# Three raw weight pieces and two stores go from SyncE's DMA queue to GpSimd's; a row load, a table part and two step A groups move to later pairs

## The chip, the cores and the metric

The kernel runs on one core of a Trainium2 chip. A core has a matrix engine (TensorE, PE in the profile), VectorE (DVE), ScalarE (ACT), GpSimd (POOL) and SyncE (SP, which here only issues transfers). Each engine works through its own instructions in order and waits for the others by semaphores. Transfers are issued by SP, ACT or POOL, each into a DMA queue of its own (q1, q10 and q0 in the profile), and all queues are served by the same 16 DMA engines. The metric is device time in microseconds (us); lower is better.

## The reference, cut to what matters

```python
X = np.fft.rfft(x, axis=1)                     # x: 4 x 3008 x 256
Yr = Xr @ w_r - Xi @ w_i + b_r                 # mixing of the 256 channels, per frequency
Yi = Xr @ w_i + Xi @ w_r + b_i
Y = soft_threshold(Yr, 0.01) + 1j * soft_threshold(Yi, 0.01)
y = np.fft.irfft(Y, n=3008, axis=1)            # 12032 tokens x 256
h = y @ w_in                                   # 256 -> 2048
g = np.maximum(h, 0.0) + alpha * np.minimum(h, 0.0)
out = g @ w_out                                # 2048 -> 256
```

## The kernel before, in words

The sequence length is factored as 3008 = 47 x 64, and each batch passes five steps. Step A (`a_load`, `a_mm`, `a_evac`) is a length 47 transform over rows of x. Step B (`b_load`, `b_mm`, `b_evac`) is the length 64 transform with a table `rb_s`. The mixing with w_r and w_i (`m_mm`, `m_evac`) follows, then the inverse transforms C (`c_mm`, `c_evac`, table `cf_s`) and D (`d_mm`). The 24 frequency slots are handled as 12 pairs. Behind the transforms stand the two large products with w_in and w_out, which take most of the time. This change touches only the first tenth of the program: the first batch, and what is loaded meanwhile.

The order of all work is written out by hand. A loop over t = 0 to 12 issues for each t: step B of pair t, `b_load` of pair t+3, the store of pair t-4, mixing of pair t-1, step C of pair t-3, and then extra work. The extra work has four parts that matter here.

- **Raw weight pieces.** w_in and w_out arrive as 16 pieces of 512 KB each (`conv_load`, line 257), w_in and w_out in turn; they are numbered 0 to 15 here. Three of them fit into the upper half of `cw_s`, so piece n+3 can be issued only when piece n has been read. `pump` then splits each piece into a high and a low part with some ten ACT and DVE instructions. L272 on ACT is the first to read a piece, L286 on ACT the last; L292 on DVE reads it too. From t = 2 on, three or four such groups are issued in each t.
- **Table parts.** `load_rb` (line 208) loads the table of step B: slots 4 to 11 during step A, 12 to 17 and 18 to 23 in the loop. Pair t needs slots 2t and 2t+1, so pair 6 is the first to need slots 12 to 17.
- **The next batch's step A.** `a_load(1, g)` loads 376 KB of x; its four matmuls for two groups are run with pair 4, or, in the change, with pair 6. `a_evac` on ACT copies each group out of PSUM, and `put` stores the results (192 KB each).
- **Step B's inputs.** Each `b_load` is two transfers of 128 KB issued by POOL; POOL also runs one small instruction (L511, writing `Xl`) for each pair, on which the mixing of that pair waits.

Everything that one engine issues is in program order, its transfers included: a transfer that waits for its buffer holds up the transfers behind it on that queue.

Of the kernel before, what the change touches and what calls it, by code (L numbers as in the profile page):

```python
# [96 lines left out]
def fft_mix_moe(ctx, tc, x, w_r, w_i, b_r, b_i, w_in, w_out, alpha, la, rb, lc, rd, lf, cf, sel, out):  # L97
    nc = tc.nc
# [61 lines left out]
    def half(h):  # L160
        t = const.tile([128, 2, FH * 2 * C], F32R, tag=f"half{h}", name=f"w{h}")
        wi_h[h] = t[:, 0].rearrange("p (w k f) -> p w k f", w=2, k=CT)
        wo_h[h] = t[:, 1].rearrange("p (m w f) -> p m w f", w=2, f=C)

    def load_tables():
        nc.sync.dma_start(out=rd_s, in_=rd)
        nc.sync.dma_start(out=alpha_s, in_=alpha.rearrange("(k p) -> p k", p=128))
# [39 lines left out]
    def load_rb(n0, n1, at=0):  # L207
        nc.sync.dma_start(out=rb_s[:, n0:n1], in_=rb[:, n0 + at:n1 + at])

    def load_cf(n0, n1):  # L210
        nc.gpsimd.dma_start(out=cf_s[:, n0:n1], in_=cf[:, n0:n1])
# [34 lines left out]
    conv_deep = [1]  # L246
    conv_raw, conv_old, conv_ops = [], [], []

    def conv_load():

        m, i = divmod(conv_m[0], 2)
        conv_m[0] += 1
        k = conv_m[0] % 3
        raw = cw_s[:, NSLOT + 8 * k:NSLOT + 8 * k + 8].rearrange("p (k n) f -> p k (n f)", k=2)
        raw = raw.rearrange("p k (n w) -> p k n w", w=2)
        src = w_out.bitcast(U32)[256 * m:256 * m + 256] if i else w_in.bitcast(U32)[:, 512 * m:512 * m + 512]
        nc.sync.dma_start(out=raw.rearrange("p k n w -> p k (n w)"), in_=src.rearrange("(k p) f -> p k f", p=128))
        conv_raw.append((raw, m, i))

    def conv_first(raw, m, i):  # L260
# [48 lines left out]
    def conv_fetch():  # L309
        assert not conv_ops  # L310
        while len(conv_raw) < conv_deep[0] and conv_m[0] < conv_m[1]:
            conv_load()

    def pump(n):

        while n > 0:
            if not conv_ops:
                conv_fetch()
                second = conv_second(*conv_old.pop()) if conv_old else []
                first = conv_first(*conv_raw.pop(0)) if conv_raw else []  # L320
                first, second = ([(op,) for op in ops] for ops in (first, second))
                if first and second:
                    conv_ops.extend([second[0] + first[0], first[1], second[1], second[2] + second[3] + first[2]])
                else:
                    conv_ops.extend(first + second)
                if not conv_ops:
                    return
            for op in conv_ops.pop(0):
                op()
            n -= 1  # L330
# [5 lines left out]
    def put(*queues):  # L336
        for n, (o, i) in enumerate(stores):
            (queues or (nc.sync,))[n % max(len(queues), 1)].dma_start(out=o, in_=i)
        stores.clear()
# [3 lines left out]
    def a_load(b, g):  # L343

        if g == 0:
            ad[b] = dram.tile([NQ, R, C], F32, tag="ad", name=f"ad{b}")
        src = x[b].rearrange("(p r) c -> p r c", r=R)[:, 4 * g:4 * g + 4]
        if b == 0:
            ts = [x_s[:, 4 * g:4 * g + 4]]
        elif b == 1 and g in X1_TAGS:  # L350
            tags = X1_TAGS[g]
            ts = [work.tile([NP, 4 // len(tags), C], F32, tag=tag, name="xt", bufs={"Yl": None, "gl": 3}.get(tag, 1))
                  for tag in tags]
        else:
            ts = [work.tile([NP, 4, C], F32, tag="xt", name="xt")]
        if (b, g) == (0, 0):
            ts = [ts[0][:, 0:2], ts[0][:, 2:4]]
        n = 4 // len(ts)
        for i, t in enumerate(ts):

            for p in ((0, 80), (80, NP)):
                nc.sync.dma_start(out=t[slice(*p)], in_=src[slice(*p), n * i:n * i + n])
        xt[b, g] = ts
# [20 lines left out]
    def a_mm(b, g):  # L384
        ps = ps_f.tile([NQ, 2, C], F32, tag="f", name="ps_a")
        pa[b, g] = ps
        if b < 2:
            ts = x_rows(b, g)
            n = 2 // len(ts)
            for i, t in enumerate(ts):  # L390
                PE.matmul(ps[:, n * i:n * i + n], lf_s, t, start=True, stop=True)  # L391
            return
        hi, lo = xp.pop((b, g))
        PE.matmul(ps, la_s[:, 0], hi, start=True, stop=False)
        PE.matmul(ps, la_s[:, 1], hi, start=False, stop=False)
        PE.matmul(ps, la_s[:, 0], lo, start=False, stop=True)

    def a_evac(b, g):
        ps = pa.pop((b, g))
        if b == 0:  # L400
            st = a0_s[:, g]
        else:
            tag = A1_TAGS[g] if b == 1 and g < len(A1_TAGS) else "zst"
            st = work.tile([NQ, 2, C], F32, tag=tag, name="ast", bufs={"bt": 3, "zst": 3, "Yt": 1, "Yc": 1}.get(tag))
        if b == 0 and g % 2:
            V.tensor_copy(out=st, in_=ps)
        else:
            A.activation(out=st, in_=ps, func=AF.Copy)
        if b:
            stores.append((ad[b][:, 2 * g:2 * g + 2], st))  # L410
# [3 lines left out]
    def b_half(q, h):  # L414
        if h == 0:
            bt[0, q] = work.tile([128, 2, C], F32, tag="bt", name="bt", bufs=3)
        src = a0_s.rearrange("(w s q) (h g) r c -> q h w s (g r) c", w=4, s=2, h=2)[q, h]
        for k in range(2):
            (nc.sync if h else nc.gpsimd).dma_start(out=bt[0, q][64 * h:64 * h + 64, k], in_=src[:, k])

    def b_load(b, q):
        if (b, q) == (0, 2):
            t = work.tile([128, 2, C], F32, tag="Yc", name="bt2", bufs=1)
        else:
            t = work.tile([128, 2, C], F32, tag="bt", name="bt", bufs=3)
        if b == 0:
            src = a0_s.rearrange("(w s q) g r c -> q w s (g r) c", w=4, s=2)[q]
        else:
            src = ad[b].rearrange("(w s q) r c -> q w s r c", w=4, s=2)[q]

        for k in range(2):
            (nc.gpsimd if b == 0 else nc.sync).dma_start(out=t[:, k], in_=src[:, k])
        bt[b, q] = t
# [550 lines left out]
    NG = R // 2  # L984
    EARLY = 4
    FILL = 14
    C0 = 1
    PT = [0, 0, 3, 3, 3, 3, 3, 3, 3, 3, 3, 4]
    TAIL = [['me', 1], ['ce', 3], ['cm', 2], ['cm', 1], ['ce', 2], ['ce', 1], ['d'], ['f', 4], ['e'], ['f', 6]]
    WARM = 38  # L990
# [10 lines left out]
    with tc.manual_schedule():  # L1001
# [13 lines left out]
        for n, (b, g) in enumerate(seq):  # L1015
            a_mm(b, g)
            if n >= 1:
                a_evac(*seq[n - 1])
            if n == NG // 2:
                b_half(0, 0)  # L1020
                b_half(1, 0)
            if n == NG:
                b_half(0, 1)
                b_half(1, 1)
                load_rb(4, 12)
                for _ in range(C0):
                    conv_load()
                a_load(1, 1)
                bias_parts()
                b_load(0, 2)  # L1030
        a_evac(*seq[-1])
# [4 lines left out]
        def run(fn, q, *args):  # L1036
            if 0 <= q < NPAIR:
                fn(0, q, *args)
# [10 lines left out]
        for t in range(NPAIR + 1):  # L1049
            if t == 0:  # L1050
                first_pair()
            elif t > 1:
                run(b_mm, t)
            run(b_load, t + 3)
            run(c_evac, t - 4)
            if t > 1:
                run(b_evac, t)
            run(m_evac, t - 2)
            if t > 1:
                run(m_mm, t - 1, ps_h)  # L1060
            for g in range(2, EARLY) if t == 4 else ():
                a_mm(1, g)
                a_evac(1, g)
            if t:
                run(b_evac2, t)
            run(c_mm, t - 3)
            if t < NPAIR:
                pump(PT[min(t, len(PT) - 1)])
            if t in (3, 5):
                load_rb(3 * t + 3, 3 * t + 9)  # L1070
            if t in (0, 3, 6, 8):
                load_cf((t + 1) // 3 * 6, (t + 1) // 3 * 6 + 6)
            if t == 2:
                put()
                conv_load()
                conv_deep[0] = 2
            if t == 5:
                put()
            if t == 6:
                load_tables()  # L1080
            if 7 <= t < 12:
                a_load(1, t - 5)
            if t == NPAIR - 1:
                load_rb(0, 4)
            if t == 10:
                half(1)
                conv_m[1] = FT
# [160 lines left out]
        for k in range(len(spairs) + SLAG):  # L1248
# [7 lines left out]
            if k >= SLAG:  # L1256
                n, t = spairs[k - SLAG]
# [45 lines left out]
```

## Time and profile before

| | |
|---|---|
| median of 3 runs | 1335.99 us (1335.87 to 1336.71) |
| the profiled execution | 1338.1 us, of which the span from first to last instruction is 1336.0 us |
| granted TensorE clock, mean | 0.997 |
| PE / DVE / ACT / POOL busy | 1321.9 / 1046.0 / 732.7 / 352.8 us |
| bytes over the DMA queues | 89.74 MB |

The profiled execution took 2.1 us more than the median of the runs, about as much as lies outside its span. Places in the trace are given in us from the start of the span. Steps A to C of the first batch lie between 9 and 91 us, and the large products begin at about 104 us.

### The profile page before, as it was taken

The page shows a single profiled execution, that of the slowest core. Times are in us where ns is not written, and L with a number is a line of the kernel's source. Part 1 is how long each engine was busy: PE and PEld are TensorE (multiplying, and loading weights), DVE is VectorE, ACT ScalarE, POOL GpSimd, SP SyncE. Part 2 cuts the span into 40 slices and gives each one's busy share as a digit, 9 for nine tenths or more (in the row PEclk, how much of TensorE's full clock was granted, in tenths as well). Part 3 has the DMA queues.
Part 4 walks back from the last instruction along what each step waited for, and adds up shares of the span by engine and source line. Part 5 has one row for each costly group of instructions (what it writes and reads, how often), then busy time and mean ns, then how long its engine had stood idle before and what let it go on. Part 6 is the DMA issues. An engine that isn't in the chain of part 4 may idle for free.

```text
span 1336.0 us, 22138 instructions
## 1 busy us (share of the span) xinstructions
PE 1321.9 (99%) x7864; PEld 1156.1 (87%) x7864; DVE 1046.0 (78%) x1874; ACT 732.7 (55%) x1453; POOL 352.8 (26%) x337
## 2 busy tenths in 40 slices
PE   8999999999999999999999999999999999999998
PEld 5978878888888888888879888988898889888987
DVE  3666866777787877686878888888888888888885
ACT  3666654555455544444455555555555555555554
POOL 3403752212221222222222222222222222222222
PEclk9999999999999999999999999999999999999999
DMA  9984333432143322121101101110111011101000
GB/s 204 254 232 138 102 108 97 129 107 87 57 144 101 107 70 67 57 76 36 37 13 40 28 11 30 29 29 11 31 29 28 12 29 29 29 12 29 17 16 25
DMA packets 103759, 89.74 MB, mean 67 GB/s; under 512 B 62446, under 2 KB 85849, under 8 KB 103648
## 3 DMA queue, kind: packets, MB, share of 16 engines
q1 hardware_dynamic: 95744, 77.68, 20.7%
q0 software_dynamic: 4912, 7.76, 2.3%
q10 hardware_dynamic: 2992, 2.88, 0.7%
q8 instruction: 62, 1.02, 0.3%
q14 instruction: 49, 0.40, 0.1%
HBM read 50.76 MB, written 34.34 MB: 64 GB/s over the span
## 4 chain that ended last, share of the span: by engine, by line
PE 89%; DVE 4%; DMA 3%; ACT 1%; issue 1%; SPq 0%; ACTq 0%; DVEq 0%
PE ps_h L725 36%; PE ps_o L752 10%; PE ps_o L750 10%; PE ps_o L751 10%; PE ps_m L547 6%; PE ps_d L646 4%; PE ps_b L437 3%; PE ps_o L919 3%; PE ps_a L391 2%; DVE q L737 1%; PE ps_m L534 1%; DMA cw_s<-in_moe_w_out 1%; PE ps_c L615 1%; PE ps_c L616 1%; DMA rb_s<-tab_rb 1%
## 5 line engine op out<-in xcount | busy, mean ns | idle before, releaser
L725 PE MATMUL ps_h<-yh,w 128*128 128x512 f32 (+1 forms) x1472 | 492.5, 389 | 2.3 <-DVE q L737 1.4
L725 PEld LDWEIGHTS ps_h<-yh,w 128*128 128x128 f32 x1472 | 275.1, 188 | 58.2 <-DVE q L737 4.5
L725 PE MATMUL ps_h<-yl,w 128*128 128x512 f32 (+1 forms) x736 | 284.8, 387 | 0.0
L853 POOL TENSOR_TENSOR l<-t,h 128x512 fp32r<-128x512 f32 x98 | 126.9, 1295 | 448.8 <-ACT h L851 423.8
L824 DVE SCALAR_TENSOR_TENSOR sq<-sq,beta_s,ps_h 128x512 f32<-128x512 f32 (+1 forms) x240 | 166.2, 724 | 58.6 <-ACT sq L823 58.3
L739 ACT ACTIVATE gh<-q 128x512 fp32r<-128x512 f32 x144 | 91.0, 632 | 159.4 <-DVE q L737 159.4
L742 POOL TENSOR_TENSOR gl<-q,gh 128x512 fp32r<-128x512 f32 x69 | 93.5, 1355 | 270.9 <-ACT gh L739 216.1
L725 PEld LDWEIGHTS ps_h<-yl,w 128*128 128x128 f32 x736 | 138.9, 189 | 21.7 <-DVE yl L697 0.2
L737 DVE SCALAR_TENSOR_TENSOR q<-q,beta_s,ps_h 128x512 f32<-128x512 f32 x144 | 107.0, 743 | 59.3 <-ACT q L736 58.1
L823 ACT ACTIVATE sq<-ps_h 128x512 f32<-128x512 f32 (+1 forms) x240 | 132.0, 577 | 31.3 <-PE ps_h L725 27.9
L839 ACT ACTIVATE dh<-sq 128x768 fp32r<-128x768 f32 x98 | 83.0, 847 | 108.2 <-DVE sq L824 81.7
L736 ACT ACTIVATE q<-ps_h 128x512 f32<-128x512 f32 x144 | 85.3, 592 | 79.1 <-PE ps_h L725 76.9
L851 ACT ACTIVATE h<-t 128x512 fp32r<-128x512 f32 x98 | 62.0, 633 | 104.6 <-DVE t L849 102.5
L750 PE MATMUL ps_o<-gh,w 128*128 128x512 f32 x288 | 114.6, 398 | 0.0
L751 PE MATMUL ps_o<-gh,w 128*128 128x512 f32 x288 | 112.7, 391 | 0.0
L752 PE MATMUL ps_o<-gl,w 128*128 128x512 f32 x288 | 112.7, 391 | 0.0
L848 DVE TENSOR_TENSOR dl<-sq,dh 128x768 fp32r<-128x768 f32 x98 | 93.2, 951 | 0.0
L742 DVE TENSOR_TENSOR gl<-q,gh 128x512 fp32r<-128x512 f32 x75 | 59.2, 789 | 42.3 <-ACT gh L739 41.3
L752 PE MATMUL ps_o<-l,sw_a 128*128 128x256 f32 x294 | 82.7, 281 | 0.0
L750 PE MATMUL ps_o<-h,sw_a 128*128 128x256 f32 x294 | 82.0, 279 | 0.0
L845 DVE TENSOR_TENSOR t<-sq 128x512 f32<-128x512 f32 x98 | 67.7, 691 | 2.9
L852 DVE TENSOR_TENSOR l<-t,h 128x512 fp32r<-128x512 f32 x98 | 67.0, 684 | 0.0
(202 smaller groups left out, 2946.2 us busy)
## 6 DMA issues: line engine op xcount, KB each, us to landing
zt<-zd SPq DMA_DIRECT2D x32, 384.0 KB
zd<-zst SPq DMA_DIRECT2D x37, 256.0 KB
ad<-ast SPq DMA_DIRECT2D x48, 192.0 KB
bt<-ad SPq DMA_DIRECT2D x72, 128.0 KB
out<-oT SPq DMA_DIRECT2D x248, 32.0 KB
xt<-in_x SPq DMA_DIRECT2D x21, 320.0 KB
cw_s<-in_moe_w_in SPq DMA_DIRECT2D x8, 512.0 KB
cw_s<-in_moe_w_out SPq DMA_DIRECT2D x8, 512.0 KB
```

The lines of the kernel that those rows point to most:

```text
L725: PE.matmul(ps, wi_h[m // FH][:, w, ct, 128 * (m % FH):128 * (m % FH) + 128], a[ct][:, 0:n], start=(k == 0), stop=(k == 3 * CT - 1))
L736: A.activation(out=q, in_=ps, func=AF.Relu, scale=-1.0)
L737: V.scalar_tensor_tensor(out=q, in0=q, scalar=beta_s[:, m:m + 1], in1=ps, op0=ALU.mult, op1=ALU.add)
L739: A.activation(out=hi, in_=q, func=AF.Copy)
L742: return lambda: (V if by_v else G).tensor_tensor(out=lo, in0=q, in1=f(hi), op=ALU.subtract)
L750: PE.matmul(o, wh, gh, start=first, stop=False)
L751: PE.matmul(o, wl, gh, start=False, stop=False)
L752: PE.matmul(o, wh, gl, start=False, stop=last)
L823: A.activation(out=q[:, j], in_=ps, func=AF.Relu, scale=-1.0)
L824: V.scalar_tensor_tensor(out=q[:, j], in0=q[:, j], scalar=beta_s[:, m:m + 1], in1=ps, op0=ALU.mult, op1=ALU.add)
L848: V.tensor_tensor(out=dl, in0=q[:, HS:], in1=f(dh), op=ALU.subtract)
L853: G.tensor_tensor(out=l24, in0=t24, in1=f(h24), op=ALU.subtract)
```

## The change

Pieces 0, 1 and 2 are no longer issued by SP during and after step A, but by POOL, with pairs 1, 2 and 3. The two stores of the next batch's first step A groups go from SP at t = 2 to POOL at t = 3. `a_load(1, 1)` moves from step A to t = 4, and `load_rb(12, 18)` from t = 3 to t = 4, behind it; the matmuls of groups 2 and 3 move from t = 4 to t = 6, and their stores from t = 5 to t = 7. `load_rb(18, 24)` stays at t = 5. The number of bytes, matmuls and split operations is the same.

```diff
-    def conv_load():
+    def conv_load(queue=None):
...
-        nc.sync.dma_start(out=raw.rearrange("p k n w -> p k (n w)"), in_=src.rearrange("(k p) f -> p k f", p=128))
+        (queue or nc.sync).dma_start(out=raw.rearrange("p k n w -> p k (n w)"), in_=src.rearrange("(k p) f -> p k f", p=128))
...
                 load_rb(4, 12)
-                for _ in range(C0):
-                    conv_load()
-                a_load(1, 1)
                 bias_parts()
...
-            for g in range(2, EARLY) if t == 4 else ():
+            for g in range(2, EARLY) if t == 6 else ():
                 a_mm(1, g)
                 a_evac(1, g)
             if t:
                 run(b_evac2, t)
             run(c_mm, t - 3)
+            if t in (1, 2, 3):
+                conv_load(nc.gpsimd)
             if t < NPAIR:
                 pump(PT[min(t, len(PT) - 1)])
-            if t in (3, 5):
-                load_rb(3 * t + 3, 3 * t + 9)
+            if t == 4:
+                a_load(1, 1)
+            if t in (4, 5):
+                load_rb(6 * t - 12, 6 * t - 6)
             if t in (0, 3, 6, 8):
                 load_cf((t + 1) // 3 * 6, (t + 1) // 3 * 6 + 6)
-            if t == 2:
-                put()
-                conv_load()
+            if t == 3:
+                put(nc.gpsimd)
                 conv_deep[0] = 2
-            if t == 5:
+            if t == 7:
                 put()
```

On SP, the place is behind the table part for slots 4 to 11 (the first row) up to the part for slots 12 to 17 (the last). Rows with L257 are raw pieces, L362 is the load of x, and L338 are the two stores.

```order
 L208 DMA rb_s<-tab_rb 128x1024
-L257 DMA cw_s<-in_moe_w_in 128x2x512
-L362 DMA xt<-in_x 80x1024
-L362 DMA xt<-in_x 14x1024
-L338 DMA ad_158<-ast 96x512 x2
-L257 DMA cw_s<-in_moe_w_out 128x2x512
-L257 DMA cw_s<-in_moe_w_in 128x2x512
+L257 DMA cw_s<-in_moe_w_out 128x2x512
+L362 DMA xt<-in_x 80x1024
+L362 DMA xt<-in_x 14x1024
 L208 DMA rb_s<-tab_rb 128x768
```

Seven transfers leave the stretch. Piece 3 (the w_out row that is left), which stood behind the last row shown, now comes directly behind the first, and the load of x and the table part stand behind it.

On POOL, these are the rows from the small `Xl` instruction of pair 1 to that of pair 4, before the change. L432 are step B's inputs, L211 a part of step C's table.

```order
L511 TENSOR_SCALAR Xl<-Xl 128x4x64
L432 DMA bt<-a_83 128x1x256 x2
L511 TENSOR_SCALAR Xl<-Xl 128x4x64
L432 DMA bt<-a_83 128x1x256 x2
L511 TENSOR_SCALAR Xl<-Xl 128x4x64
L211 DMA cw_s<-tab_cf 128x768
L432 DMA bt<-a_83 128x1x256 x2
L511 TENSOR_SCALAR Xl<-Xl 128x4x64
```

The same stretch after the change:

```order
L511 TENSOR_SCALAR Xl<-Xl 128x4x64
L257 DMA cw_s<-in_moe_w_in 128x2x512
L432 DMA bt<-a_83 128x1x256 x2
L511 TENSOR_SCALAR Xl<-Xl 128x4x64
L257 DMA cw_s<-in_moe_w_out 128x2x512
L432 DMA bt<-a_83 128x1x256 x2
L511 TENSOR_SCALAR Xl<-Xl 128x4x64
L257 DMA cw_s<-in_moe_w_in 128x2x512
L211 DMA cw_s<-tab_cf 128x768
L338 DMA ad_158<-ast 96x512 x2
L432 DMA bt<-a_83 128x1x256 x2
L511 TENSOR_SCALAR Xl<-Xl 128x4x64
```

Each of pieces 0 to 2 stands behind the `Xl` instruction of its pair, and piece 2, the table part and the two stores now stand ahead of the inputs of pair 7.

On ACT, this is the end of pair 4 before the change: the soft threshold (L560), the two copies out of step A (L408), the first reading of piece 2 (L272), and the next pair's copy out of step C with its store.

```order
L560 ACTIVATE Yc<-ps_m,lam_s 128x512
L408 ACTIVATE ast<-ps_a 96x512 x2
L272 ACTIVATE conv<-cw_s 128x512
L626 ACTIVATE zst<-ps_c 128x512
L630 DMA zd_453<-zst 128x2x256
```

And the end of pair 6 after it, where the same two copies stand now:

```order
L560 ACTIVATE Yc<-ps_m,lam_s 128x512
L408 ACTIVATE ast<-ps_a 96x512 x2
L286 ACTIVATE conv<-cw_s 128x512
L287 ACTIVATE w_245<-conv 128x2x256
L626 ACTIVATE zst<-ps_c 128x512
```

The two copies have moved behind the threshold of pair 6's turn and ahead of L286, the last reading of piece 2, for which SP's issue of piece 5 waits.

## Rows read from the trace of the kernel before

**Rows 1.** The page: busy time of each engine, and the chain that ended last.

```profile
PE 1321.9 (99%) x7864; PEld 1156.1 (87%) x7864; DVE 1046.0 (78%) x1874; ACT 732.7 (55%) x1453; POOL 352.8 (26%) x337
...
PE 89%; DVE 4%; DMA 3%; ACT 1%; issue 1%; SPq 0%; ACTq 0%; DVEq 0%
```

**Rows 2.** Busy time by stretch (start:end, length, engines, PEclk, DMA share, GB/s).

```profile
24.00:32.00 8.00, 5.99 (x49) 5.64 (x50) 2.28 (x6) 2.13 (x7) 2.94 (x5) 1.00 1.04 219
...
31.90:35.30 3.40, 3.40 (x16) 3.30 (x16) 0.56 (x2) 1.60 (x4) 1.78 (x3) 0.51 1.04 229
...
44.00:48.00 4.00, 4.00 (x25) 2.96 (x24) 2.11 (x5) 3.17 (x7) 0.95 (x2) 1.00 1.06 225
```

**Rows 3.** The chain of waits, in order of time (start, us, what).

```profile
23.11 8.50 DMA rb_s<-tab_rb
...
46.33 1.72 PE ps_a L391 x4
...
56.91 12.72 DMA cw_s<-in_moe_w_out
...
91.51 8.59 PE ps_a L391 x20
```

**Rows 4.** Timeline of PE: start, length, instruction, idle before it and releaser.

```profile
30.03 0.68 PE L437 MATMUL ps_b<-rb_s,bt 128*128 128x128 f32 x4 [0.87 <-DMA bt<-a]
...
31.74 1.86 PE L437 MATMUL ps_b<-rb_s,bt 128*128 128x128 f32 x8 [1.03 <-DMA rb_s<-tab_rb]
...
53.59 1.05 PE L437 MATMUL ps_b<-rb_s,bt 128*128 128x128 f32 x8
...
58.42 1.05 PE L437 MATMUL ps_b<-rb_s,bt 128*128 128x128 f32 x8
...
83.75 0.50 PE L525 MATMUL ps_m<-bias_p,ones 128*128 128x512 f32 x1 [0.72 <-DVE Y L561]
```

**Rows 5.** Timeline of ACT, same columns.

```profile
42.89 0.67 ACT L272 ACTIVATE conv<-cw_s 128x512 f32<-128x512 f32 x1 [2.98 <-DMA cw_s<-in_moe_w_out]
43.47 0.67 ACT L286 ACTIVATE conv<-cw_s 128x512 f32<-128x512 uint16 x1
...
45.16 0.39 ACTq L630 DMA_DIRECT2D zd<-zst  x1
...
69.66 0.68 ACT L272 ACTIVATE conv<-cw_s 128x512 f32<-128x512 f32 x1 [3.52 <-DMA cw_s<-in_moe_w_out]
```

**Rows 6.** Timeline of SP's queue: issue, its length, transfer.

```profile
23.63 0.63 SPq L257 DMA_DIRECT2D cw_s<-in_moe_w_in  x1
...
31.62 0.35 SPq L208 DMA_DIRECT2D rb_s<-tab_rb  x1
44.16 0.37 SPq L257 DMA_DIRECT2D cw_s<-in_moe_w_out  x1
```

**Rows 7.** Timeline of POOL.

```profile
32.44 0.40 POOL L511 TENSOR_SCALAR Xl<-Xl 128x256 fp32r<-128x256 f32 x1 [5.14 <-DVE Xl L508]
...
36.56 0.49 POOL L511 TENSOR_SCALAR Xl<-Xl 128x256 fp32r<-128x256 f32 x1 [2.17 <-DVE Xl L508]
...
41.33 0.77 POOL L511 TENSOR_SCALAR Xl<-Xl 128x256 fp32r<-128x256 f32 x1 [1.21 <-DVE Xl L508]
```

**Rows 8.** DMA queues from 24 to 32 us: packets, MB, share; one issue to landing.

```profile
q1 hardware_dynamic: 549, 1.26, 72.8%
q0 software_dynamic: 412, 0.49, 30.9%
...
cw_s<-tab_cf POOLq DMA_DIRECT2D x1, 384.0 KB, 12.0
```

**Rows 9.** DMA queues from 44 to 49 us.

```profile
q0 software_dynamic: 422, 0.79, 75.3%
q1 hardware_dynamic: 160, 0.34, 28.7%
```

**Rows 10.** DMA queues from 54 to 58 us.

```profile
q1 hardware_dynamic: 498, 1.07, 83.0%
```

More of the change, by code (lines that the diff above doesn't have):

```diff
@@ L986, in fft_mix_moe @@
     FILL = 14
-    C0 = 1
     PT = [0, 0, 3, 3, 3, 3, 3, 3, 3, 3, 3, 4]
```

## The prediction

> **What bounds the kernel now.** I read the page first: PE is busy 99% of the span and carries 89% of the chain that ended last [rows 1]. So a change in the first tenth is worth what it moves the moment at which PE finishes the pairs, at 91.5 us, where the chain enters step A of the next batch [rows 3]; behind that PE is nearly always busy, so a shift there should reach the end undiminished.
>
> Next I read PE's timeline over the pairs. Pair 6 begins at 53.59 and pair 7 at 58.42, so a pair costs PE 4.83 us [rows 4]. PE waits in few places. It waits 0.87 us for the inputs of pair 1, and 1.03 us for the table part of slots 4 to 11, which frees pair 2 at 31.74 [rows 4]. Behind these two waits the granted clock is 0.51 for 3.40 us, its lower level [rows 2]: at half speed 3.40 us do what 1.70 us do at full speed, so about 1.7 us are lost. Together that is 0.87 + 1.03 + 1.70 = 3.6 us, the most that the early part can give. Late in the loop there is one more wait, 0.72 us [rows 4].
>
> Then the queues. From 24 to 32 us all 16 engines are busy (share 1.04) and move 219 GB/s [rows 2]; SP's queue moved 1.26 MB of it and POOL's 0.49 [rows 8]. From 44 to 49 us it is the reverse: POOL's queue moved 0.79 MB and SP's only 0.34 [rows 9], and ACT's queue, whose store was issued at 45.16 [rows 5], has no row there at all. So a transfer's arrival depends on what stands in the other queues. Last, ACT: it waits 2.98 us until 42.89 for piece 1 and 3.52 us until 69.66 for piece 5 [rows 5], whose landing is 12.72 us of the chain [rows 3]. ACT's waits reach PE only late; the splitting has some slack.
>
> **The change, part by part.**
>
> *What leaves SP early.* Piece 0 (23.63 [rows 6]), the load of x, two stores, and pieces 1 and 2 go: 3 x 0.52 + 0.385 + 0.39 = 2.34 MB. They stood behind the table part, so they delayed it only by sharing engines. Of SP's 1.26 MB from 24 to 32 us [rows 8] some 0.65 MB were the table part and last inputs, so about 0.6 MB were of this kind; at 219 GB/s that is 2.8 us of engine time. It would cover the waits of 0.87 and 1.03 us, and perhaps the low clock. Bounds: 0 (the engines that finished last had none of the removed work) and 3.6 us; I take 2.0, the two waits.
>
> *Pieces 0 to 2 on POOL.* POOL's issue time is hidden: POOL waits 5.14, 2.17 and 1.21 us for DVE ahead of its `Xl` instructions [rows 7]. But piece 0 now leaves POOL only behind the one of 32.44 and piece 1 behind that of 36.56 [rows 7]; each 2 us sooner if PE is 2 us sooner, so piece 1 leaves at about 35. A POOL transfer of 384 KB took 12.0 us with SP's queue full [rows 8]. With SP's queue empty I take half, 6 us (an estimate from that row), so piece 1 lands at about 41 instead of 42.9. The bounds are 39 and 43. ACT reads it, then reads piece 0 for the last time, 0.57 + 0.67 us later (42.89, 43.47 [rows 5]).
>
> *The table part of slots 12 to 17.* This is the term that decides. Before, it was issued at 31.62 [rows 6], 22 us before pair 6 used it at 53.59 without a wait [rows 4]. Now it stands on SP behind piece 3 and the load of x. Piece 3 overwrites piece 0, so it waits for ACT's last reading; before it went out at 44.16 [rows 6], now at about 42.5. Ahead of the end of the table part SP's queue then holds 0.52 + 0.385 + 0.39 = 1.30 MB. At the same time POOL's queue gets piece 2, a table part of step C, two stores and the inputs of pair 7, 0.52 + 0.39 + 0.39 + 0.26 = 1.56 MB, beginning about 41 (its `Xl` instruction was at 41.33 [rows 7], now some 1.5 us sooner).
>
> The price of SP's 1.30 MB has two bounds. At SP's rate of 24 to 32 us (1.26 MB in 8 us, 157 GB/s [rows 8]) it takes 8.3 us, so about 51.3 with half a microsecond to start. At the rate of 44 to 49 us, SP gets 68 GB/s while POOL's queue, at 158 GB/s [rows 9], needs 9.9 us for its 1.56 MB, until about 51; SP has by then moved 0.55 MB, and the other 0.75 MB follow at between 157 and 268 GB/s (1.07 MB in 4 us when SP's queue was nearly alone [rows 10]), so 53.8 to 55.8, and 57 with ACT's stores between. The situation is nearer to the second row, since POOL's queue holds large transfers in both; but the removed load before 41 leaves the engines emptier. I take 53.5.
>
> When does PE want it? The four step A matmuls (1.72 us [rows 3]) no longer stand ahead of pair 6, and PE is 2.0 us early: 53.59 - 1.72 - 2.0 = 49.9. So PE waits about 3.6 us at pair 6, a wait that was not there before. What is late next is pair 6's mixing, and behind it the four matmuls that now follow it.
>
> *The sum.* Pair 7 begins at 53.5 + 4.83 + 1.72 = 60.05. A wait of 3.6 us is longer than the two that preceded the low clock in rows 2, so I add half of that loss, 0.9 us (bounds 0 and 1.7): 60.95 against 58.42 before, +2.5. At the end of the loop the 0.72 us at 83.75 [rows 4] should go, since ACT then has more time for the late pieces: +2.5 - 0.7 = +1.8 us.
>
> *The rest.* The two copies on ACT now wait for the moved matmuls ahead of the last reading of piece 2, so piece 5 is issued some 5 us later than at 56.91 [rows 3]. I cost this at nothing, because PE is later too and the stores that stood ahead of piece 5 (0.39 MB) now stand behind it; without that cover, ACT's 3.52 us at 69.66 [rows 5] would grow, and a part of it would reach PE. The copy of step C's pair 1 on ACT now may wait for a store issued about 43.5; the one issued at 45.16 had not started by 49 [rows 5, 9]. That puts ACT at 50 to 51, still ahead of PE's 53.5. A changed issue cost on SP or POOL is 0.4 to 0.7 us each, on engines with idle time.
>
> The profiled execution took 1338.1 us, 2.1 above the median; its span would become 1337.8, and the median 1335.99 + 1.8 = **1337.8 us**.
>
> **The rivals.**
>
> *Slower: POOL's queue holds SP's up for longer.* If the division of 44 to 49 us [rows 9] lasts until POOL's queue is empty, the table part lands at 55.8 to 57, and pair 7 begins 2.3 to 3.5 us later than in my sum: +4.1 to +5.3 us, 1340 to 1341.3. It decides from a landing at about 54.4, where the sum passes +2.7. For it: ACT's store, which did not move for 4 us. Against: SP's 157 GB/s earlier.
>
> *Faster: the table part is there in time.* If SP's queue runs at 268 GB/s as from 54 to 58 us [rows 10], its 1.30 MB take 4.9 us and land at about 48, before PE's 49.9. Then the early gain stays: -2.0 - 0.7 = -2.7, and with the low clock gone too -4.4, so 1331.6 to 1333.3. Against it stands that POOL's queue was almost empty in rows 10 and will hold 1.56 MB. The Trainium skill speaks for this rival: "DMA: Bandwidth & Descriptors", section Anatomy of one DMA, gives 2.0 us plus bytes at 436 GB/s for a transfer on GpSimd's path. By it a 384 KB transfer takes 2.9 us and 1.30 MB about 5.0 us, an estimate, so no wait at pair 6 and about -2.7 us in all; this trace does not agree under load, with 12.0 us for such a transfer [rows 8].
>
> *No effect: the early gain and the wait cancel.* With the table part at 51.3 and full clock, pair 7 begins at 57.85, -0.6, and the late pieces hold the loop's end as before: 1335.4 to 1336.5. For it: ACT's wait of 3.52 us for piece 5 shows the splitting close to the bound.
>
> **How the numbers follow.** A measurement of this kernel can tell about 0.2%, 2.7 us, from no change. The forecast (+0.6 to +2.7) gets 0.40, no effect 0.09, the slower rival 0.36, the faster one 0.15. So faster 0.15, same 0.49, slower 0.36. Cutting one in ten at either end, and allowing for the bounds of the landing, gives 1333 to 1341.3; the forecast's own range is 1336.5 to 1338.7.
>
> **What would show it.** In the changed kernel's profile: pairs 1 and 2 without waits for inputs and table (first step); the first reading of piece 1 on ACT before 42.9; SP's issue of piece 3 near 42.5; PE's pair 6 preceded by several us of idle time released by the table part, at about 53.5 (the deciding step); a half-clock stretch there instead of at 32 us; the start of pair 7 near 61; the end of step C's pairs 1 to 3 us later than 91.5. The prediction is wrong if pair 6 has no wait on the table part, or if ACT's late pieces, not PE, hold the end of the loop.

## The result, and the profile after

The changed kernel takes 1345.23 us in the median of 4 runs (1344.82 to 1346.35); beside it the kernel before took 1336.35 us (1335.87 to 1339.53, 4 runs, one more than in the table of the kernel before). The ratio is 1.0063, with an interval of 1.0045 to 1.0080, so the change costs 6 to 11 us, most likely 8 to 9. The prediction said 1337.8 us, with a range up to 1341.3. It was wrong: the time lies above its range, and beyond its slower rival. The profiled execution of the changed kernel took 1345.35 us, with a span of 1343.6 us against 1336.0 before. The profiled execution before lies 1.7 us above its median, so the two traces show 7.6 of the 8.9 us between the medians.

First PE's timeline of the changed kernel, in the places that answer to [rows 4] (start, length, instruction, idle time before it and its releaser).

```profile
29.16 0.68 PE L437 MATMUL ps_b<-rb_s,bt 128*128 128x128 f32 x4 [0.20 <-DMA bt<-a]
...
31.69 1.13 PE L437 MATMUL ps_b<-rb_s,bt 128*128 128x128 f32 x8 [1.85 <-DMA rb_s<-tab_rb]
...
48.19 0.50 PE L525 MATMUL ps_m<-bias_p,ones 128*128 128x512 f32 x1 [1.75 <-DVE Y L561]
...
57.58 2.08 PE L437 MATMUL ps_b<-rb_s,bt 128*128 128x128 f32 x8 [4.89 <-ACT zst L626]
60.20 0.80 PE L525 MATMUL ps_m<-bias_p,ones 128*128 128x512 f32 x1 [0.54 <-DVE Y L561]
...
67.64 1.05 PE L437 MATMUL ps_b<-rb_s,bt 128*128 128x128 f32 x8
```

Pair 2 begins at 31.69, against 31.74 before: the early waits give nothing. Then three waits are new: 1.75 us ahead of the mixing in pair 5's turn of the loop, 4.89 us ahead of pair 6, and 0.54 us ahead of the mixing in pair 6's turn, 7.18 us together. Pair 7 begins at 67.64 instead of 58.42, 9.2 us later. The releaser at pair 6 is no transfer: it is L626, ACT's copy of step C out of PSUM, into a buffer `zst`.

The second view is the busy time by stretch, for two stretches of [rows 2] and the one after PE's wait at pair 6 (start:end, length, engines, granted clock, DMA share, GB/s).

```profile
24.00:32.00 8.00, 5.95 (x52) 5.58 (x51) 2.63 (x6) 2.18 (x7) 3.81 (x8) 1.00 0.93 200
31.90:35.30 3.40, 3.40 (x30) 3.36 (x30) 0.91 (x2) 1.45 (x3) 2.21 (x4) 1.00 0.71 167
...
57.15:63.98 6.83, 5.86 (x24) 5.47 (x25) 4.36 (x8) 5.44 (x11) 1.86 (x3) 0.50 0.53 162
```

The stretch of low clock at 32 us is gone, but one of twice its length stands behind the wait at pair 6: 6.83 us at 0.50, the lower level of 1.2 GHz. At half speed these 6.83 us do the work of 3.4 us.

The third view is the chain of waits from 36 us on, which leads from a piece on POOL's queue to PE's wait (start, us, what).

```profile
36.14 7.07 DMA cw_s<-in_moe_w_out
...
43.23 0.04 ACT conv L272
...
44.98 0.50 ACT zst L626
...
45.50 11.35 DMA zd<-zst
...
56.93 0.61 ACT zst L626
...
58.84 0.59 ACT Yc L560
...
59.45 0.70 DVE Y L561
...
60.20 0.80 PE ps_m L525
60.99 4.22 PE ps_m L534 x24
```

Read it from the top. Piece 1 leaves POOL at 36.14 and takes 7.07 us; ACT has waited for it, splits it, and only then copies step C's pair 0 (44.98) and sends its store off (45.50). That store takes 11.35 us. Only when it has landed can ACT copy pair 1 (56.93), and behind this copy stand the soft threshold on ACT (58.84) and on DVE (59.45) on which PE's mixing at 60.20 waits. These two transfers fill 18.4 of the 24 us from 36.14 to 60.20.

Why should the copy of pair 1 wait for the store of pair 0? There are three `zst` buffers. Groups 0 and 1 of the next batch's step A were copied into two of them during step A (the tags "zst", "zst" in `A1_TAGS`). Which copy gets which buffer is settled when the program is built, and the place of the two stores in it, now at the end of pair 3, has changed that (stores_later below has the same swap from this edit alone). The waits of the two copies show it (each name is a semaphore that a transfer raises when it has landed; DMAHW5 is in both kernels the semaphore of pair 0's store; DMAHW0 and DMASW2 are those of a store of step A):

```
before   copy of pair 1: waits DMAHW0, PE     copy of pair 2: waits DMAHW5, PE
after    copy of pair 1: waits DMAHW5, PE     copy of pair 2: waits DMASW2, PE
```

So pair 1's copy and pair 2's have changed places: pair 1 now stands behind a store issued only one pair earlier, and pair 2 behind one that landed long ago (step A's two stores were there at 47.77 and 48.33). PE's pair 6 needs the PSUM buffer that the copy of pair 1 frees, since `ps_b` and `ps_c` share their buffers.

ACT's timeline shows how long it stood (columns as in [rows 5], to which the rows answer).

```profile
43.23 0.66 ACT L272 ACTIVATE conv<-cw_s 128x512 f32<-128x512 f32 x1 [3.77 <-DMA cw_s<-in_moe_w_out]
...
45.50 0.42 ACTq L630 DMA_DIRECT2D zd<-zst  x1
...
56.93 0.60 ACT L626 ACTIVATE zst<-ps_c 128x512 f32<-128x512 f32 x1 [8.96 <-DMA zd<-zst]
```

ACT does nothing for 8.96 us. The next view is the DMA queues from 24 to 32 and from 44 to 49 us, as in [rows 8] and [rows 9] (packets, MB, share).

```profile
q0 software_dynamic: 830, 0.96, 59.0%
q1 hardware_dynamic: 273, 0.65, 34.1%
...
q0 software_dynamic: 408, 1.19, 68.9%
q1 hardware_dynamic: 223, 0.46, 27.4%
```

Early, SP's queue moves 0.65 MB instead of 1.26, and POOL's 0.96 instead of 0.49: the room that was made went to POOL's queue. From 44 to 49 us ACT's queue again has no row, so the store of 45.50 had not begun, as the one of 45.16 had not before. That one landed at 53.02, 7.86 us after its issue; this one took 11.35 us.

The landings can be read from the semaphore events in the trace. For four transfers of the changed kernel (issue, queue, transfer, from which to which time its 16 parts landed, us from issue):

```
36.14  POOL  piece 1                        39.97 to 43.21   7.07
45.50  ACT   store of step C's pair 0       52.68 to 56.84  11.35
46.19  SP    table part, slots 12 to 17     52.87 to 56.50  10.30
44.95  POOL  second input of pair 7         50.89 to 56.67  11.72
```

So the table part landed at 56.50, 3 us later than predicted and only 0.3 us ahead of the store. Pair 6 had two waits side by side; the trace names the later one.

How long the store of pair 0 is on its way goes with the two stores of step A. In the eight kernels of this document that have them on POOL in pair 3 it took 8.45 to 11.86 us, in the six others 6.13 to 8.68 us.

### The profile page after: what moved, and what is told of

Its sections match the earlier page's. It is cut to its first block, busy times and chain, and to the rows that moved or that the text cites. A ratio compares the mean times of both kernels' runs of the same rounds, so it can differ in the third digit from the quotient of the medians.

```text
span 1343.6 us, 22138 instructions
## 1 busy us (share of the span) xinstructions
PE 1324.0 (99%) x7864; PEld 1157.7 (86%) x7864; DVE 1046.3 (78%) x1874; ACT 734.3 (55%) x1453; POOL 356.3 (27%) x342
## 4 chain that ended last, share of the span: by engine, by line
PE 88%; DVE 5%; DMA 3%; issue 2%; ACT 2%; SPq 0%; ACTq 0%; DVEq 0%; POOL 0%
PE ps_h L725 36%; PE ps_o L752 10%; PE ps_o L750 10%; PE ps_o L751 10%; PE ps_m L547 6%; PE ps_d L646 4%; PE ps_o L919 3%; PE ps_b L437 3%; PE ps_a L391 2%; DVE q L737 1%; DMA zd<-zst 1%; PE ps_m L534 1%; PE ps_c L615 1%; PE ps_c L616 1%; DMA xt<-in_x 1%
```

## The experiments

The first theory was formed from these rows: two things hold PE at pair 6 (they are called locks below), the late table part and the buffer, and each alone is enough; the pieces on POOL cost nothing, as the prediction said. The first four kernels test it by undoing either lock, both, and by moving the pieces alone. The kernel before took 1336.89 us beside these four (21 runs).

**table_early.** The changed kernel, with the table part back in pair 3.

```diff
-            if t in (4, 5):
-                load_rb(6 * t - 12, 6 * t - 6)
+            if t in (3, 5):
+                load_rb(3 * t + 3, 3 * t + 9)
```

> The changed kernel with one part undone: the table part of slots 12 to 17 is issued with pair 3 again, ahead of piece 3 and the load of x. Theory of two locks (pair 6 is held both by that table part, landed at about 56.5 us, and by ACT's copy out of step C, which waits 8.96 us for a buffer whose store lands at 56.8): ACT's wait remains, pair 6 still begins after 54 us, time 1342 to 1346. Rival, the table part alone (the step on which the prediction rested): the wait at pair 6 goes, pair 6 begins near 50 to 52 us, time 1334 to 1338.

Measured: 1344.56 us, ratio 1.0054 (1.0039 to 1.0069). PE's timeline at pair 6, and ACT's:

```profile
56.44 1.37 PE L437 MATMUL ps_b<-rb_s,bt 128*128 128x128 f32 x8 [3.80 <-ACT zst L626]
```

```profile
55.79 0.60 ACT L626 ACTIVATE zst<-ps_c 128x512 f32<-128x512 f32 x1 [5.17 <-DMA zd<-zst]
```

The table part is there in time, and PE still waits 3.80 us for the copy. The table alone is not the cause. (Piece 0 landed at 40.12 here instead of 37.44, and PE begins pair 5 1.9 us later than in the changed kernel, 1.23 us of it in a wait for DVE; so the shorter wait at pair 6 is no gain.)

**buffer_free.** The changed kernel, with step A's two results in a buffer of their own, so that the three `zst` are step C's alone.

```diff
-            st = work.tile([NQ, 2, C], F32, tag=tag, name="ast", bufs={"bt": 3, "zst": 3, "Yt": 1, "Yc": 1}.get(tag))
+            st = work.tile([NQ, 2, C], F32, tag=tag, name="ast", bufs={"bt": 3, "zst": 3, "gh": 3, "Yt": 1, "Yc": 1}.get(tag))
...
-    A1_TAGS = ("zst", "zst", "Yt", "zst", "bt", "bt", "bt", "Xh", "Xl", "Xh", "Xl", "zst", "zst", "Yc")
+    A1_TAGS = ("gh", "gh", "Yt", "zst", "bt", "bt", "bt", "Xh", "Xl", "Xh", "Xl", "zst", "zst", "Yc")
```

> The changed kernel with one wait taken away: the first two results of the next batch's step A are kept in another buffer (one that is idle until the large products), so step C's copies find a free buffer and no longer wait for a store. Theory of two locks: the table part still lands at about 55 to 57 us and holds pair 6 there, time 1341 to 1345. Rival, the buffer alone: pair 6 begins near 50 to 52 us, time 1334 to 1338.

Measured: 1341.35 us, ratio 1.0037 (1.0025 to 1.0049). PE's timeline at pair 6:

```profile
56.59 2.05 PE L437 MATMUL ps_b<-rb_s,bt 128*128 128x128 f32 x8 [4.33 <-DMA bt<-a]
```

No wait for `zst` is left, but PE begins pair 6 at 56.59, nearly as late as in the changed kernel (57.58). The trace names an input transfer (bt); by the semaphore events the table part landed at 56.46, and pair 6's own inputs at 42.74 and 43.34, so it is the table part. This lock costs 4.33 us where the other is gone.

**both_undone.** Both edits together.

> Both of the edits before, in the changed kernel. Theory of two locks: pair 6 begins at 50 to 52 us without a wait of more than 1 us, the clock stays at its upper level, time 1333 to 1338. Rival, the crowded queues as such (pieces on GpSimd's queue make every transfer of 40 to 57 us late, whichever it is): pair 6 or 7 waits for something else, time 1340 or more.

Measured: 1337.45 us, ratio 1.0008 (0.9998 to 1.0017). PE's timeline from pair 6:

```profile
51.66 1.08 PE L437 MATMUL ps_b<-rb_s,bt 128*128 128x128 f32 x8
54.20 0.50 PE L525 MATMUL ps_m<-bias_p,ones 128*128 128x512 f32 x1 [1.46 <-DVE Y L561]
```

Pair 6 begins at 51.66 without a wait. With both locks open the time is that of before, within what can be measured. That the clock would stay at its upper level did not come true: it was low for 3.41 us from 32.02 on.

**pieces_alone.** The kernel before, with pieces 0 to 2 issued by POOL in pairs 1 to 3 and nothing else of the change.

```diff
-                for _ in range(C0):
-                    conv_load()
...
+            if t in (1, 2, 3):
+                conv_load(nc.gpsimd)
...
-                conv_load()
+            if t == 3:
                 conv_deep[0] = 2
```

> The kernel before with one part of the change: pieces 0 to 2 are issued by GpSimd with pairs 1 to 3; stores, the load of x, table parts and step A groups stay where they were. Theory of two locks: the pieces alone cost nothing, since stores and table part go out early: 1333 to 1337. Rival, the pieces: ACT's waits for pieces 0 and 1 (3.10 and 3.77 us in the changed kernel) reach PE, 1339 to 1343.

Measured: 1340.07 us, ratio 1.0022 (1.0013 to 1.0031). ACT's and PE's timeline:

```profile
40.99 0.67 ACT L272 ACTIVATE conv<-cw_s 128x512 f32<-128x512 f32 x1 [6.58 <-DMA cw_s<-in_moe_w_in]
```

```profile
43.77 0.50 PE L525 MATMUL ps_m<-bias_p,ones 128*128 128x512 f32 x1 [2.11 <-DVE Y L561]
```

This part of the theory fell. Piece 0 leaves POOL at 31.88, only behind the `Xl` instruction of pair 1, and lands at 40.97; ACT waits 6.58 us for it, and the soft threshold behind it on ACT and DVE makes PE wait 2.11 us, with the lower clock from 44.65 to 48.06. So the pieces cost some 3 us, in the range of the rival, and there were at least three causes. (Its profiled execution, at 1339.35 us, lies 0.7 below the median.) In both_undone the pieces were as late in the order, but piece 0 landed at 39.53, 1.4 us sooner, with x and the two stores out of the early queue; and PE was 1.2 us later there (pair 4 at 41.77 instead of 40.61) after its own low clock at 32 us. Together that is more than the 2.11 us, and PE had no such wait.

The next four kernels take single parts of the change alone, and move the pieces one pair sooner. The kernel before took 1336.90 us beside them (33 runs).

**pieces_sooner.** As pieces_alone, with the three issues in pairs 0, 1 and 2.

```diff
-            if t in (1, 2, 3):
+            if t in (0, 1, 2):
                 conv_load(nc.gpsimd)
```

> The kernel with the pieces alone on POOL (1340.07, 3.2 us over before), its three issues one pair sooner: pairs 0, 1 and 2 instead of 1, 2 and 3. Theory (POOL runs in order: piece 0 stands behind the Xl instruction of pair 1, 31.5, and so arrives at 41): piece 0 goes out at about 26 and piece 1 at 32, ACT's wait of 6.58 us for piece 0 and PE's wait of 2.11 us with its half clock disappear, 1336 to 1337.5. Rival (the engines were full from 24 to 32 us, and what POOL's queue gets there delays the inputs of pairs 1 to 3, which are on the same queue behind it): PE waits 1.5 to 3 us more for bt at pairs 1 to 3, and the half clock is at 32 us again, 1338.5 to 1341.

Measured: 1337.29 us, ratio 1.0005 (0.9996 to 1.0014). ACT's timeline at the first reading of piece 0:

```profile
35.03 0.70 ACT L272 ACTIVATE conv<-cw_s 128x512 f32<-128x512 f32 x1 [1.57 <-DMA cw_s<-in_moe_w_in]
```

Piece 0 now leaves at 25.00 and ACT waits 1.57 us for it. The price of the pieces is gone, although the same bytes stand in the same queue: what cost was POOL's order, with the piece behind an instruction that itself waits. The rival fell too; PE waits 0.28 us for the inputs of pair 1 and 0.72 us for those of pair 4, not 1.5 to 3 us.

**stores_later.** The kernel before, with the two stores on POOL in pair 3.

```diff
             if t == 2:
-                put()
                 conv_load()
+            if t == 3:
+                put(nc.gpsimd)
                 conv_deep[0] = 2
```

> The kernel before with one edit: the two stores of step A's results go from SP in pair 2 to POOL in pair 3. Theory (lock of the buffer): ACT's copy of step C's pair 1 now waits for the store of pair 0, issued at 45.16 and about 8 us on its way, so it ends at about 53.6 instead of 49.8; PE's pair 6 needs it at 53.6, so PE waits 0 to 1 us there; 1336 to 1338. Rival (the engines, relieved of 0.39 MB at 27 to 41 us, bring pieces 1 and 2 sooner, so that the lock costs nothing and ACT's wait of 2.98 us shrinks): 1334.5 to 1336. Second rival (the stores on POOL ahead of the inputs of pair 7 make the store of pair 0 land at 56 to 57 as in the changed kernel): PE waits 3 to 4 us, 1339.5 to 1341.

Measured: 1340.01 us, ratio 1.0021 (1.0012 to 1.0030). ACT's, DVE's and PE's timeline:

```profile
52.52 0.60 ACT L626 ACTIVATE zst<-ps_c 128x512 f32<-128x512 f32 x1 [2.02 <-DMA zd<-zst]
...
54.32 0.69 ACT L560 ACTIVATE Yc<-ps_m,lam_s 128x512 f32<-128x512 f32 x1
```

```profile
55.04 0.69 DVE L561 SCALAR_TENSOR_TENSOR Y<-ps_m,Yc 128x512 f32<-128x512 f32 x1 [4.08 <-ACT Yc L560]
```

```profile
55.79 0.50 PE L525 MATMUL ps_m<-bias_p,ones 128*128 128x512 f32 x1 [1.49 <-DVE Y L561]
...
76.55 0.50 PE L525 MATMUL ps_m<-bias_p,ones 128*128 128x512 f32 x1 [1.03 <-DVE Y L561]
...
82.69 0.51 PE L525 MATMUL ps_m<-bias_p,ones 128*128 128x512 f32 x1 [0.92 <-DVE Y L561]
```

The lock shows alone, without the rest of the change, and it costs more than the theory gave it (1336 to 1338). The time lies in the range of the second rival, but not by its mechanism: the store of pair 0 landed at 52.44, not at 56 to 57, and PE begins pair 6 at 53.24 without a wait. The theory said that PE needs the PSUM buffer only at 53.6; but the copy also stands on ACT ahead of the soft threshold (L560), DVE waits 4.08 us for that, and PE 1.49 us for DVE. ACT's lateness also sends the later pieces out late, which gives 1.03 and 0.92 us more. Together 3.44 us, against 0.72 before [rows 4]: 2.7 more, of the 3.1 measured. (The edit also raises `conv_deep` one pair later, so piece 2 is issued behind the table part and not ahead of it; late_stores_buffers keeps this and has no price, so it is not the cause.)

**table_later.** The kernel before, with the table part of slots 12 to 17 in pair 4, behind piece 3.

> The kernel before with one edit: the load of the table part of slots 12 to 17 goes from pair 3 to pair 4, so it stands on SP behind piece 3 (issued at 44.16) instead of ahead of piece 2. Theory (it lands late only because pieces, x, stores and inputs stand with it in the queues at 44 to 47 us): SP has 0.91 MB to move from 44.2 on, piece 3 landed at 52 before, so the table part lands at 52 to 55 and PE, ready at 53.6, waits 0 to 1.5 us at pair 6; 1336 to 1338.5. Rival (its issue in pair 4 alone makes it as late as in the changed kernel, 56.5): PE waits about 3 us at pair 6, with a stretch of half clock, 1339.5 to 1341.

Measured: 1337.37 us, ratio 1.0002 (0.9993 to 1.0011). The table part was issued at 43.32 and landed at 51.67, a little sooner than expected. PE begins pair 6 without a wait:

```profile
52.23 1.05 PE L437 MATMUL ps_b<-rb_s,bt 128*128 128x128 f32 x8
```

Its place alone costs nothing.

**groups_alone.** The kernel before, with groups 2 and 3 of step A in pair 6 and their stores in pair 7.

> The kernel before with one edit: the step A groups 2 and 3 of the next batch go from pair 4 to pair 6, and their stores from pair 5 to pair 7. Theory (two locks at pair 6, the groups themselves are innocent): PE's pair 6 begins 1.7 us sooner, at about 51.9, the groups take the 1.7 us back ahead of pair 7, which begins at 58.4 as before; same time, 1336 to 1337.5. Rival 1 (the groups' later place was a gain that the locks hid, since the kernel with both locks undone was 2.6 us below the kernel with the pieces alone): pair 7 or the end of the pairs comes 1.5 to 2.5 us sooner, 1334 to 1335.5. Rival 2 (the two copies, now ahead of the last reading of piece 2 on ACT, send piece 5 out later, and ACT's wait at 69.66 grows by some 3 us): 1338 to 1340.

Measured: 1336.22 us, ratio 0.9992 (0.9983 to 1.0000). PE begins pair 6 at 51.89 and pair 7 at 58.45, as the theory said: the groups cost and give nothing that can be told.

The last four close the gaps: is the price of late stores the buffer alone, what makes the table part late, and does a kernel with all three causes gone return to before or pass it? The kernel before took 1336.46 us beside them (33 runs).

**late_stores_buffers.** As stores_later, with the buffers of buffer_free.

> The kernel with the stores alone moved to POOL in pair 3 (1340.01, +3.1), with one more edit: the two results of step A that they store lie in a buffer of their own (three of the name gh, as in the kernel with the buffers free), so that step C's copies have all three of theirs. Theory (the price of late stores is the buffer alone): ACT's copy of pair 1 has no wait for the store of pair 0 and ends near 48.5, PE's waits of 0.9 to 1.5 us for DVE at 55.8, 76.6 and 82.7 go, 1336 to 1337.5. Rival (the price is what POOL's stores add to the queues at 40 to 50 us: later pieces, later inputs): little changes, 1339 to 1340.5.

Measured: 1336.56 us, ratio 0.9998 (0.9989 to 1.0007). The two stores still go out from POOL in pair 3, and the 3 us are gone. ACT copies pair 1 at 48.46 without a wait:

```profile
48.46 0.58 ACT L626 ACTIVATE zst<-ps_c 128x512 f32<-128x512 f32 x1
```

The price was the buffer.

**x_early.** As buffer_free, with the next batch's x loaded in step A as before, so that only piece 3 stands ahead of the table part on SP.

```diff
                 load_rb(4, 12)
+                a_load(1, 1)
...
-            if t == 4:
-                a_load(1, 1)
```

> The kernel with the buffers free (1341.35; table part of slots 12 to 17 still in pair 4, 4.33 us wait at pair 6) with one more edit: the next batch's rows of x are loaded in the prologue again, as before, so only piece 3 stands ahead of the table part on SP. Theory (the table is late because of what stands with it in the queues, x above all, since moving it alone cost nothing): it lands 2 to 4 us sooner, at 52.5 to 54.5, PE's wait at pair 6 falls from 4.33 to 1 to 2.5 us, 1338 to 1340. Rival (the pieces and stores on POOL hold it, x does not matter): it lands at 56 and the time stays at 1340.5 to 1342.

Measured: 1339.01 us, ratio 1.0018 (1.0009 to 1.0027), in the range of the theory. The table part was issued at 44.69 and landed at 49.40, 7 us sooner than in buffer_free and sooner than the theory gave (52.5 to 54.5), and pair 6 has no wait for it. But x is not all that differs: POOL issued piece 2 at 44.41 here, just behind SP's piece 3 (44.26), and at 42.30 in buffer_free, 1.5 us ahead of it (43.79). Piece 3, which stands ahead of x on SP, took 3.59 us instead of 6.50. So the runs don't separate x from the order of the two queues. Nor is it shown what the 2.5 us over before are: the pieces are still in pairs 1 to 3, but in both_undone too, which is only 0.6 us over. (The profiled execution took 1341.86 us, the longest of the 10 runs, so its later waits aren't read here.)

**mended.** The changed kernel with all three causes gone: the buffers of buffer_free, the table part in pair 3, the pieces in pairs 0, 1 and 2.

> The changed kernel with all three causes taken away: step A's two results in a buffer of their own, the table part loaded in pair 3, the three pieces on POOL in pairs 0, 1 and 2. Left of the change: pieces and stores on POOL, x in pair 4, the groups in pair 6. Theory (three causes, no fourth): as the kernel before, 1335.5 to 1337. Rival 1 (x and the two stores, out of the way from 24 to 41 us, are then a gain): 1333 to 1335. Rival 2 (piece 0 ahead of the inputs of pair 3 on POOL costs, and stores and x at 44 us delay piece 2): 1337.5 to 1339.

Measured: 1335.03 us (11 runs), ratio 0.9989 (0.9980 to 0.9998). It is 0.7% below the changed kernel, 2.4 us below both_undone by the place of the pieces alone, and the lowest median of all versions. It lies between the ranges of the theory and of the first rival, and decides for neither: against the kernel before its gain is at most 0.2%, on the edge of what can be told. One wait of note is left on PE's timeline, late in the loop, behind ACT's wait of 4.29 us for a piece (until 75.69); the profiled execution was the longest of the 11, so the wait may be longer here than in most:

```profile
79.50 0.51 PE L525 MATMUL ps_m<-bias_p,ones 128*128 128x512 f32 x1 [1.85 <-DVE Y L561]
```

**groups_and_pieces.** The kernel before with the edits of groups_alone and pieces_sooner.

> The kernel before with two edits, each of which made no difference that could be told: the groups in pair 6 with their stores in pair 7, and the three pieces on POOL in pairs 0, 1 and 2. Theory (neither touches what ends last): 1335.5 to 1337.5. Rival (together they gain, since the wait of 0.83 us that the copies of the groups brought to PE in the kernel with the pieces sooner goes with the groups, and the half clock at 32 us was gone there): 1333.5 to 1335.

Measured: 1336.34 us, ratio 1.0003 (0.9994 to 1.0012). The rival, a gain of the two together, fell. The little that mended has beyond it, if it is more than noise, can then come from x or the stores out of the early queue; the stores gave nothing alone (late_stores_buffers), and x in pair 4 was not tried alone.

## Why the prediction was wrong

The step that failed is in the part on the rest: the copy of step C's pair 1 "now may wait for a store issued about 43.5 [...] That puts ACT at 50 to 51, still ahead of PE's 53.5", costed at nothing. The wait was seen; its length was not. The store went out at 45.50, 2 us later than assumed, and took 11.35 us; ACT came free at 56.93. The step gave it some 7 us, about what the store of 45.16 had taken (7.86 us, with nothing moved by 49 [rows 5, 9]), as if what the change adds to the queues at that time could not make it slower. The step also looked only at PSUM. The soft threshold stands behind the copy, so ACT's lateness reaches DVE and PE by a second way; stores_later shows some 3 us by that way, with PE's pair 6 begun in time at 53.24. Undoing this buffer alone brought the changed kernel down by 3.9 us, undoing the table part alone, the term that was to decide, by 0.7.

Then the other steps, in their order.

*What leaves SP early: 2.0 us, measured 1.65, but for another reason.* Pair 5 begins at 45.38; before it was 48.75, less 1.72 for the groups 47.03. None of it comes from the two waits on which the step was built: 0.87 and 1.03 us [rows 4] are now 0.20 and 1.85. The working took 0.6 MB at 219 GB/s for time that the table part would gain. But the room went to POOL's queue, and the table part of slots 4 to 11, 512 KB, took 7.98 us instead of 8.50 [rows 3]. In all 14 profiled executions it was issued between 22.75 and 23.69 and landed between 30.66 and 31.97, whatever else stood on SP. The 1.65 us are about what the low clock at 32 us costs before (1.7), and its absence is no shown work of the change: five of the 14 profiled executions have this stretch and nine have not, and of two kernels that are the same as before up to 31 us one has it (groups_alone) and one has not (table_later).

*Pieces 0 to 2 on POOL: costed at nothing, measured about 3 us alone.* The path was followed to POOL's issue, but then only piece 1 was timed (41, landed 43.21). Piece 0 was thought early enough: it moved from 23.63 [rows 6] to 32, and in pieces_alone ACT stands 6.58 us for it. In the changed kernel piece 1 is the link: ACT reads it at 43.23 after 3.77 us, and the store that decides leaves behind it.

*The table part: 53.5, measured 56.50.* This term was too small by 3 us. Here the slower rival was right in its landing (55.8 to 57) and in its order of size, and buffer_free shows its price, 4.33 us of wait. The late transfer is a matter of company: behind piece 3 alone it came in time (table_later, x_early); with x ahead of it and pieces and stores on POOL it took 10.30 us. The rival's reason, that POOL's queue holds SP's up, has this for it: piece 3 on SP took 3.59 to 3.72 us in the four kernels where piece 2 left POOL within 0.2 us of it, and 6.50 and 7.67 us in buffer_free and the changed kernel, where piece 2 had left 1.5 and 2.9 us ahead. No run separates this from x.

The Trainium skill ("DMA: Bandwidth & Descriptors", section Anatomy of one DMA), by whose fit for a transfer on GpSimd's path the prediction gave the faster rival a price, would have 2.9 us for 384 KB, an estimate. The trace does not agree under load: it shows 10.30 us for this one on SP's queue, and 4.81 us for one of 384 KB that POOL issued at 42.41. With the engines at a share of 0.33 a store of 256 KB on ACT's queue, issued at 57.55, took 2.12 us.

*PE ready for pair 6 at 49.9, measured 52.5* (its last work ahead of it, step C's matmuls, begins at 51.66 and takes 0.86 where nothing is in the way). The mixing in pair 5's turn begins 2.0 us late, as PE waits for DVE, behind ACT's wait for piece 1, and ends 2.3 us late; the early gain was 0.35 smaller.

*The clock: 0.9, measured 3.4 us* (6.83 us at half), 1.7 more than before. The form was right, a long wait at pair 6 with low clock behind it; the size that was predicted was a quarter of it.

*The end of the loop: -0.7, confirmed.* No wait is left between 61 and 96 us where there were 0.72 [rows 4]; the delay of 9.2 us at pair 7 shrinks to 8.1 at the end of the pairs, where the chain enters step A at 99.62 and not at 91.51 [rows 3], and 7.6 us of that are left in the spans. Piece 5 was costed right as well: it is issued at 68.15 instead of 56.91, 9.2 of these 11.2 us are PE's own delay, and PE has no wait for it.

The sum of the trace: new waits 7.18, 0.15 more at pairs 1 and 2, and 1.7 more of low clock make 9.0 us, against 9.2 measured at pair 7. By causes the sum isn't additive. Undoing the table part alone gave 0.7 us, the buffer alone 3.9, both 7.8 (differences of the medians 1345.23, 1344.56, 1341.35 and 1337.45; 0.7 is less than these intervals can tell): locks that stand side by side hide one another. Done alone on the kernel before, the late stores cost 3.1 and the pieces 3.2, the table part and the groups nothing that can be told.

Two things stay open. Why ACT's store had to stand for 3.5 us and more before anything of it moved is not shown: the rows tell that from 44 to 49 us the other two queues moved 1.65 MB, not by which rule. And how much x, and how much the order of the two queues, has to do with the late table part is not shown either.

## What to carry to other kernels

A store that is moved changes who gets its source buffer and when; before costing it at nothing, read in the built program whom each copy now waits for, and what stands behind that copy on its engine. A transfer moved to a compute engine's queue leaves when the instruction ahead of it is done, so its time is that instruction's, not the loop step's: one pair sooner was worth 2.8 us. And when a trace shows one wait, ask what else has only just landed; here the table part landed 0.3 us ahead of the store that was named. With the other lock gone the table part costs 3.9 us and the buffer 7.1 (1341.35 and 1344.56 against 1337.45); in the changed kernel undoing them gave only 0.7 and 3.9.

## What the runs showed of the hardware that was not expected

Room on one DMA queue was not given to the transfer that waited there. With half of the bytes gone from SP's queue (0.65 MB instead of 1.26 from 24 to 32 us) the 512 KB table part still took 7.98 us, and between 7.2 and 8.8 us in every profiled execution, and POOL's queue moved twice as much.

A queue can be left out for long. ACT's 256 KB store, issued at 45.50, took 11.35 us in the changed kernel, and up to 49 us its queue moved nothing that the view shows, while the 16 engines moved 332 GB/s.

How fast the engines were when they were full differed with the packets. In the changed kernel they moved 200 GB/s at a share of 0.93 from 24 to 32 us, where 655 of 1103 packets were under 512 B, and 332 GB/s at 0.96 from 44 to 49 us, where 156 of 631 were. That the size of the packets is the cause was not tested. Still, a number of bytes taken from one stretch does not price another.
